# Convolution taps laid out by pairs of channels, with the two channels innermost

## The chip, the cores and the metric

The kernel runs on one core of a Trainium2 chip. The metric is device time in microseconds (us), the median of several runs. Engines are named as in the profile: PE is TensorE, DVE VectorE, ACT ScalarE, POOL GpSimd, and SP the engine that only issues transfers here. All data are float32 or rounded float32 (fp32r).

## The reference

The result mixes two branches of the same length, gated per row: a state-space convolution (an FFT in the reference) over 2048 samples and 512 channels, and a dense layer pair with gelu.

```python
g = sigmoid((u * gate_w).sum(-1, keepdims=True))            # [L, 1], L = 2048
K = einsum("dn,dnl,dn->dl", C, exp(dt * A * l), dt * B).real # taps, d = 512, n = 128
a = irfft(rfft(pad(u)) * rfft(pad(K)))[:L] + u * Dskip       # causal convolution
b = gelu(x @ w1 + b1) @ w2 + b2                              # x: 2048 x 512, w1: 512 x 1792
out = g * a + (1 - g) * b
```

The part that matters here is K: for each channel a sum over 128 states (the partitions) of products of a complex coefficient with a complex power, at 2048 sample numbers. The kernel splits a sample number into 32 coarse and 64 fine steps, so that K of one channel is a product of two tables, 32 x 128 by 128 x 64.

## The kernel before

The program has two halves. `front` makes the taps, runs the first transform stage of taps and signal, and does the whole dense branch between them; `conv` then multiplies the spectra, transforms back and adds the branches. Between the halves the first stage's results go through DRAM (`tu_d` for the signal, `tk_d` for the taps), since their rows change places.

In `front` every piece of work is a task of a planner (`Plan`) with an engine, an estimated duration, a due time out of the table DUES and the names of what it reads and writes. The planner's result is a fixed order of instructions on each engine; engines take their instructions strictly in that order and wait on semaphores where another engine has to be done first. Dense work (matmuls at lines 985 to 987 and 1028 to 1031, gelu at 1002, splits into high and low parts at 1005 and 1012) and tap work are interleaved on PE, ACT and DVE in that order.

The taps come in 4 groups of 128 channels, each in 4 chunks of CW = 32 channels, so 16 chunks. For one chunk:

- `phases` (DVE, L695 and L703) adds up 33 integer phases per channel by doubling, into `ph`, and `waves` (ACT, L711 to L713) turns them into cosines and sines in `tt`.
- `begin` (ACT, L721) copies the first four powers from `x4` into `xc[k]` (two such buffers lie in the tile den), and `powers` doubles them three times with complex products (`cmul`, DVE, L594 to L597) to 32 coarse powers. The products' temporaries `xt_` and `xv_` lie in the tile loft, as `tt` does; `zz` holds the factors.
- `magnitudes` (POOL's memset L740, DVE L752 and L750) makes 64 fine magnitudes by doubling, in both directions from the middle, and `rotate` (DVE L763, L770, L774) multiplies them by cosines and sines into `y`.
- `contract` multiplies the two tables on PE (L788): per channel two matmuls (real, imaginary), with 32 coarse powers as the weights and 64 fine samples as the moving data. Four channels stand side by side in columns of 32. A matmul's output goes to every eighth word of a PSUM tile `pks`. Each f32 matmul is two matmul records and two weight loads in the profile, so a chunk has 128 records of each; this text calls them a burst.

Behind a burst DVE adds the skip term (L804), ACT copies the result out (L807), and after every second chunk the first transform stage follows (PE L489, ACT L815). After the fourth chunk of a group eight transfers store it to `tk_d` (L830, on SP's queue, which also loads the signal's rows for the second half, L535). `conv` loads tk (L1197) and multiplies it with constants (p2k, L1218).

Before the change the channel is the innermost index of all the tables of a chunk: `y` is [2, 64, CW], `xc` [2, 32, CW], `tt` [2, 33, CW], and a factor of `cmul` is a run of 32 channels that is read again for each sample. A matmul of `contract` therefore reads its channel at a step of 32 words:

```python
x[:, r, :, ch],
y[:, r, :, ch],
```

Of the kernel before, what the change touches and what calls it, by code (L numbers as in the profile page):

```python
# [17 lines left out]
P = 128  # L18
# [331 lines left out]
def gated_mix(  # L350
# [52 lines left out]
    def front(pool, psum, keep, attic, loft, den, pr):  # L403
# [29 lines left out]
        pus = tiles(N_PU, [P, D], "pu", space=psum)  # L433

        sk = pool.tile([P, 64, 2, 4, 8], F32, name="sk")
        y = pool.tile([P, 2, 64, CW], F32, name="y")
        xc = [den[:, k : k + 4].rearrange("p k d -> p (k d)").rearrange("p (a b c) -> p a b c", a=2, c=CW) for k in (0, 4)]
        xt_, xv_ = (loft[:, k * 1024 : k * 1024 + 1024].rearrange("p (a b c) -> p a b c", a=2, c=CW) for k in range(2))
        tt = loft[:, 2048:4160].rearrange("p (a b c) -> p a b c", a=2, c=CW)
        ph = pool.tile([P, 33, CW], I32, name="phase")  # L440
        zz = pool.tile([P, 2, 5, UW], F32, name="zz")
        x4 = pool.tile([P, 2, 4, UW], F32, name="x4")
        ea = tiles(2, [P, 6, UW], "ea")
        dtb = pool.tile([P, UW], F32, name="dtb")
        ti = pool.tile([P, UW], I32, name="ti")
# [95 lines left out]
        def make_dt():  # L541

            x, k, r, ki = dts
            ki = ki.bitcast(I32)
            ln2h = 355.0 / 512.0
            v = nc.vector

            def before():
                v.tensor_scalar(k, x, 1.0 / np.log(2.0), MAGIC, ALU.mult, ALU.add)
                v.tensor_scalar(k, k, MAGIC, None, ALU.subtract)  # L550
                v.scalar_tensor_tensor(r, k, -ln2h, x, ALU.mult, ALU.add)
                v.scalar_tensor_tensor(
                    r, k, -(float(np.log(2.0)) - ln2h), r, ALU.mult, ALU.add
                )
# [12 lines left out]
            act(0.1, lambda: nc.scalar.activation(r, r, AF.Exp, scale=0.25), -200, [], ["dt"], table="exp")
            vec(400, behind, -200, [], ["dt"])
            move(2, lambda: nc.sync.dma_start(dt_d.rearrange(shape, c=4), r), D_SD, ["dt"], ["dt_d"])
            some, scaled, ones = (x4[0:32, 0, k] for k in range(3))  # L570
            pl.add("POOL", 0.1, lambda: nc.gpsimd.memset(ones, 1.0), -190, [], ["x4"])
            move(16, lambda: nc.gpsimd.dma_start(some, c1[0:32, 64:192]), -190, [], ["x4"], queue="GP")
            vec(
                UW,
                lambda: v.tensor_mul(
                    scaled.rearrange("p (a b) -> p a b", b=4),
                    some.rearrange("p (a b) -> p a b", b=4),
                    r[0:32].unsqueeze(1).to_broadcast([32, 32, 4]),
                ),
                -190, ["dt"], ["x4"],  # L580
            )
            mm(
                0.4, lambda: nc.tensor.matmul(pus[1][:, 0:UW], ones, scaled, start=True, stop=True), -190,
                ["x4"], [("pu", 1)], tiled=True,
            )
            vec(UW, lambda: v.tensor_copy(dtb, pus[1][:, 0:UW]), -190, [("pu", 1)], ["dtb"])

        def cmul(due, dst, a, br, bi, n, t, v, ka, kb, kd, kt, kv):

            w = a.shape[-1]  # L590
            br = br.unsqueeze(1).unsqueeze(1).to_broadcast([P, 2, n, w])
            bi = bi.unsqueeze(1).unsqueeze(1).to_broadcast([P, 2, n, w])
            vv, m = nc.vector, n * w
            vec(2 * m, lambda: vv.tensor_mul(t, a, br), due, [ka, *kb], [kt])  # L594
            vec(2 * m, lambda: vv.tensor_mul(v, a, bi), due, [ka, *kb], [kv])  # L595
            vec(m, lambda: vv.tensor_sub(dst[:, 0], t[:, 0], v[:, 1]), due, [kt, kv], [kd])
            vec(m, lambda: vv.tensor_add(dst[:, 1], t[:, 1], v[:, 0]), due, [kt, kv], [kd])  # L597

        sc = pr[:, 0:4]
        flat = {"xt": xt_, "xv": xv_}  # L600
        fr, rr = (
            z.rearrange("p a b c -> p (a b c)").rearrange("p (k w) -> p k w", w=UW)
            for z in (xt_, xv_)
        )

        def parts(k, n, shape):

            z = xc[k].rearrange("p a b c -> p (a b c)")[:, :n]
            return z.rearrange("p (a w) -> p a w", w=UW) if shape == 1 else z

        def prepare(u, t, eb_k):
# [53 lines left out]
        def coefficients(u, t, eb_k):  # L665
# [2 lines left out]
            v = nc.vector  # L668
            vec(5 * UW, lambda: v.tensor_mul(zz[:, 0], rr[:, 2:7], eb[:, 0:5]), t, ["xv", kx], ["zz"])
            vec(5 * UW, lambda: v.tensor_mul(zz[:, 1], fr[:, 2:7], eb[:, 0:5]), t, ["xt", kx], ["zz"])  # L670
            t1, v1, wc = (eb[:, 2 * i : 2 * i + 2].unsqueeze(2) for i in range(3))
            cmul(t, wc, sc[:, 2:4].unsqueeze(2), pr[:, 4], pr[:, 5], 1, t1, v1, "pr", [], kx, kx, kx)
            cmul(t, x4[:, :, 0:1], wc, rr[:, 1], fr[:, 1], 1, t1, v1, kx, ["xt", "xv"], "x4", kx, kx)
            cmul(
                t, x4[:, :, 1:2], x4[:, :, 0:1], zz[:, 0, 0], zz[:, 1, 0], 1, t1, v1,
                "x4", ["zz"], "x4", kx, kx,
            )
            t2, v2 = (
                z.rearrange("p a b c -> p (a b c)")[:, : 4 * UW].rearrange(
                    "p (a b c) -> p a b c", a=2, b=2  # L680
                )
                for z in (xt_, xv_)
            )
            cmul(
                t, x4[:, :, 2:4], x4[:, :, 0:2], zz[:, 0, 1], zz[:, 1, 1], 2, t2, v2,
                "x4", ["zz"], "x4", "xt", "xv",
            )

# [19 lines left out]

        def waves(t):
            def sines():  # L710
                nc.scalar.activation(tt[:, 0], ph, AF.Abs)  # L711
                nc.scalar.activation(tt[:, 1], ph, AF.Sin, scale=TWO_PI / TURN)
                nc.scalar.activation(tt[:, 0], tt[:, 0], AF.Sin, bias=half_pi, scale=-TWO_PI / TURN)  # L713

            act(3.14, sines, t + D_KA, ["ph"], ["tt"], "sin")
# [1 line left out]
        def begin(c, k, t):  # L717

            cs = slice(c * CW, (c + 1) * CW)
            act(  # L720
                0.31, lambda: nc.scalar.copy(xc[k][:, :, 0:4], x4[:, :, :, cs]), t + D_KA,  # L721
                ["x4"], [("xc", k)],
            )

        def powers(c, k, t):
            cs = slice(c * CW, (c + 1) * CW)
            x = xc[k]
            for i in range(2, 5):
# [8 lines left out]
        def magnitudes(u, c, t):  # L737

            cs = slice(c * CW, (c + 1) * CW)
            pl.add("POOL", 0.1, lambda: nc.gpsimd.memset(e[:, 63], 1.0), t, [], ["y1"])  # L740

            def both(lo, step, n):

                a = e[:, lo : lo + n].copy()
                return bass.AP(a.tensor, a.offset, [a.ap[0], [step * CW, 2], *a.ap[1:]])

            def double(k):
                n = 1 << k
                an = ea[u % 2][:, k, cs].unsqueeze(1).unsqueeze(1).to_broadcast([P, 2, n, CW])
                nc.vector.tensor_mul(both(n, 64 - 3 * n, n), both(0, 64 - n, n), an)  # L750

            vec(CW, lambda: nc.vector.tensor_copy(e[:, 0], ea[u % 2][:, 5, cs]), t, [("ea", u % 2)], ["y1"])  # L752
            for k in range(5):
                vec(2 * CW << k, lambda k=k: double(k), t, [("ea", u % 2)], ["y1"])

        def rotate(t):

            v = nc.vector
            cc = tt[:, 0, 0:32]
            cc = bass.AP(cc.tensor, cc.offset, [cc.ap[0], [CW, 2], *cc.ap[1:]])  # L760

            def real():
                v.tensor_mul(  # L763
                    y[:, 0].rearrange("p (a b) c -> p a b c", a=2),
                    e.rearrange("p (a b) c -> p a b c", a=2),
                    cc,
                )

            def imag0():
                v.scalar_tensor_tensor(e[:, 0:32], e[:, 0:32], -1.0, tt[:, 1, 0:32], ALU.mult, ALU.mult)  # L770
# [3 lines left out]
            vec(32 * CW, lambda: v.tensor_mul(e[:, 32:64], e[:, 32:64], tt[:, 1, 1:33]), t, ["tt"], ["y1"])  # L774

        pair = []

        def contract(u, c, k, t):
# [4 lines left out]
            def products(g0):  # L783
                for gg in range(g0, g0 + 4):
                    for r in range(2):
                        for j in range(4):
                            ch = j * 8 + gg
                            nc.tensor.matmul(  # L788
                                pks[q][32 * j : 32 * j + 32, :, gg],
                                x[:, r, :, ch],  # L790
                                y[:, r, :, ch],
                                start=(r == 0),
                                stop=(r == 1),
                                skip_group_check=True,
# [679 lines left out]
```

## Time and profile before

| | |
|---|---|
| runs before | 509.93, 510.2 and 507.17 us; median 509.93 |
| profiled execution: span | 505.5 us, 12181 instructions; the page gives no other time for it, and the median of the runs is 4.4 us above its span |
| PE busy | 495.2 us (98%) |
| DVE busy | 429.2 us (85%) |
| ACT busy | 365.0 us (72%) |
| matmuls of L788 | 2048 records, 61.4 us busy |
| bytes moved | 107.56 MB, mean 213 GB/s |

How to read it: a group's row gives line, engine and operation, what is written and read, the shape, then busy time and mean duration of one in ns, then the idle time ahead of it and what ended that. Matmuls overlap, so a matmul's duration is longer than its distance to the next one. A stage's row gives the busy time of each engine in it; "granted clock" (PEclk) is 1.00 at full speed.

### The profile page before, as it was taken

What the parts mean: (1) busy time and instruction counts of PE and PEld (TensorE: products, weight loads), DVE (VectorE), ACT (ScalarE), POOL (GpSimd) and SP (SyncE); (2) the same over time, 40 slices, a digit from 0 to 9 for tenths busy, and PEclk for the clock granted to TensorE, in tenths of its full rate; (3) what the DMA queues carried; (4) which work ended last, traced back from release to release, by engine and by line L of the source; (5) the groups of instructions that cost most, each with busy time, mean ns of one, the idle gap of its engine ahead of it and who ended that gap; (6) DMA issues with size and microseconds to landing.
All of it is one profiled execution on the core that took longest, in us unless ns stands there. A gap on an engine that the chain in (4) does not pass through costs nothing.

```text
span 505.5 us, 12181 instructions
## 1 busy us (share of the span) xinstructions
PE 495.2 (98%) x4802; PEld 379.0 (75%) x4802; DVE 429.2 (85%) x817; ACT 365.0 (72%) x632; POOL 38.3 (8%) x78
## 2 busy tenths in 40 slices
PE   8999999999999999999999999999999999999994
PEld 7898888898989889888988888998989522222551
DVE  4977999999999999999999999999940197877455
ACT  6999997899997789997767998636834465565310
POOL 2000000000000000001010020110100100231000
PEclk9999999999999999999999999999999999999998
DMA  8978686531858622855987244950477999989897
GB/s 286 350 280 278 188 243 213 161 126 43 280 138 246 200 73 72 254 168 116 232 217 241 75 64 128 186 100 3 154 219 169 259 389 389 338 305 391 294 344 299
DMA packets 81569, 107.56 MB, mean 213 GB/s; under 512 B 39284, under 2 KB 43784, under 8 KB 80968
## 3 DMA queue, kind: packets, MB, share of 16 engines
q1 hardware_dynamic: 74792, 82.80, 51.8%
q0 software_dynamic: 6016, 20.70, 15.4%
q10 hardware_dynamic: 704, 3.28, 1.8%
q8 instruction: 38, 0.62, 0.5%
q14 instruction: 19, 0.16, 0.1%
HBM read 61.14 MB, written 45.62 MB: 211 GB/s over the span
## 4 chain that ended last, share of the span: by engine, by line
PE 93%; DMA 2%; SPq 1%; DVE 1%; issue 1%; ACT 0%; POOL 0%; DVEq 0%; POOLq 0%
PE pk L788 12%; PE ph L985 10%; PE acc L1028 10%; PE ph L987 10%; PE ph L986 10%; PE acc L1029 9%; PE acc L1031 9%; PE p2k L1218 5%; PE p2u L1218 5%; PE pa L1257 3%; PE ph L489 3%; PE pb L1373 2%; DMA tk<-tk_d 1%; SPq L830 1%; DMA tk_d<-sk 1%; PE acc L1101 1%
## 5 line engine op out<-in xcount | busy, mean ns | idle before, releaser
L985 PE MATMUL ph<-xh,wh 128*128 128x256 f32 x448 | 127.5, 285 | 0.0
L987 PE MATMUL ph<-xh,wl 128*128 128x256 f32 x448 | 126.8, 283 | 0.0
L986 PE MATMUL ph<-xlo,wh 128*128 128x256 f32 x448 | 126.7, 283 | 0.0
L985 PEld LDWEIGHTS ph<-xh,wh 128*128 128x128 f32 x448 | 85.2, 190 | 6.9 <-issue 4.0
L986 PEld LDWEIGHTS ph<-xlo,wh 128*128 128x128 f32 x448 | 85.1, 190 | 2.1
L987 PEld LDWEIGHTS ph<-xh,wl 128*128 128x128 f32 x448 | 85.2, 190 | 0.0
L1028 PE MATMUL acc<-wh,hh 128*128 128x512 f32 x208 | 84.3, 405 | 0.0
L1029 PE MATMUL acc<-wl,hh 128*128 128x512 f32 x208 | 81.7, 393 | 0.0
L1031 PE MATMUL acc<-wh,hl 128*128 128x512 f32 x208 | 81.4, 391 | 0.0
L1002 ACT ACTIVATE ph<-ph,b1t 128x256 f32<-128x256 f32 x112 | 50.5, 451 | 25.0 <-PE ph L987 23.2
L788 PE MATMUL pk<-y,den 128*32 128x64 f32 x2048 | 61.4, 290 | 0.0
L788 PEld LDWEIGHTS pk<-y,den 128*32 128x32 f32 x2048 | 57.2, 136 | 2.6 <-issue 0.7
L1012 DVE TENSOR_TENSOR hl<-ph,hh 128x512 fp32r<-128x512 f32 (+1 forms) x62 | 38.2, 618 | 18.3 <-ACT hh L1005 10.8
L1028 PEld LDWEIGHTS acc<-wh,hh 128*128 128x128 f32 x208 | 39.1, 188 | 19.4 <-issue 8.8
L750 DVE TENSOR_TENSOR y<-y,ea 128x64 f32<-128x64 f32 (+4 forms) x80 | 45.3, 566 | 0.8 <-POOL y L740 0.3
L1031 PEld LDWEIGHTS acc<-wh,hl 128*128 128x128 f32 x208 | 39.1, 188 | 8.8
L1029 PEld LDWEIGHTS acc<-wl,hh 128*128 128x128 f32 x208 | 39.1, 188 | 6.1
L1226 ACT COPY k<-p2k 128x512 f32<-128x512 f32 x32 | 18.6, 586 | 27.2 <-issue 11.3
L594 DVE TENSOR_TENSOR loft<-den,zz 128x256 f32<-128x256 f32 (+2 forms) x48 | 37.2, 774 | 0.2
L595 DVE TENSOR_TENSOR loft<-den,zz 128x256 f32<-128x256 f32 (+2 forms) x48 | 37.2, 775 | 0.1
L763 DVE TENSOR_TENSOR y<-y,loft 128x2048 f32<-128x2048 f32 x16 | 36.6, 2286 | 0.4 <-ACT loft L713 0.2
L1005 ACT CAST hh<-ph 128x512 fp32r<-128x512 f32 (+1 forms) x62 | 33.0, 533 | 4.3 <-PE acc L1029 2.4
(197 smaller groups left out, 873.3 us busy)
## 6 DMA issues: line engine op xcount, KB each, us to landing
tk_d<-sk SPq DMA_DIRECT2D x32, 256.0 KB, 5.3
t_d<-sa SPq DMA_DIRECT2D x32, 256.0 KB, 5.1
tu_d<-attic SPq DMA_DIRECT2D x40, 128.0 KB, 3.5
attic<-in_xt_dram SPq DMA_DIRECT2D x16, 256.0 KB, 4.3
attic<-in_xs_dram SPq DMA_DIRECT2D x16, 256.0 KB, 5.0
xl_d<-xlo SPq DMA_DIRECT2D x8, 512.0 KB, 5.9
xh_d<-xh SPq DMA_DIRECT2D x8, 512.0 KB, 3.9
out_dram<-io SPq DMA_DIRECT2D x16, 256.0 KB, 3.1
```

The lines of the kernel that those rows point to most:

```text
L594: vec(2 * m, lambda: vv.tensor_mul(t, a, br), due, [ka, *kb], [kt])
L750: nc.vector.tensor_mul(both(n, 64 - 3 * n, n), both(0, 64 - n, n), an)
L788: nc.tensor.matmul(pks[q][32 * j : 32 * j + 32, :, gg], x[:, r, :, ch], y[:, r, :, ch], start=(r == 0), stop=(r == 1), skip_group_check=True,)
L985: nc.tensor.matmul(p, h, xh[xk][:, d], start=(d == 0), stop=False)
L986: nc.tensor.matmul(p, h, xlo[xk][:, d], start=False, stop=False)
L987: nc.tensor.matmul(p, lo, xh[xk][:, d], start=False, stop=(d == 3))
L1002: nc.scalar.activation(phs[q][:, n], phs[q][:, n], AF.Gelu_apprx_tanh, bias=b1t[:, f : f + 1])
L1012: nc.vector.tensor_sub(lo, phs[q][:, 0:nf], hi.bitcast(F32))
L1028: nc.tensor.matmul(a, h, wh[1][w], start=start, stop=False, skip_group_check=seeded)
L1029: nc.tensor.matmul(a, h, wl[1][w], start=False, stop=False, skip_group_check=seeded)
L1031: nc.tensor.matmul(a, l, wh[1][w], start=False, stop=stop, skip_group_check=seeded)
L1218: nc.tensor.matmul(out[64 * i : 64 * i + 64], w, x, start=True, stop=True)
```

## The change

All tables of a chunk are stored by pairs of channels (CL = 2, CH = 16 pairs): pair first, then sample, then the two channels, so `y` is [2, 16, 64, 2]. `x4` is laid out so too. One channel's samples then stand 2 words apart in place of 32. The phases `ph` and the tables ea, zz and sc keep their layout; `waves` writes from one layout into the other, and a factor is read as one pair, again and again, for all samples of the pair. The core of the diff:

```diff
+CL = 2
+CH = CW // CL
...
-        y = pool.tile([P, 2, 64, CW], F32, name="y")
+        y = pool.tile([P, 2, CH, 64, CL], F32, name="y")
...
-        x4 = pool.tile([P, 2, 4, UW], F32, name="x4")
+        x4 = pool.tile([P, 2, UW // CL, 4, CL], F32, name="x4")
...
+        def each(z, n):
+            z = z.rearrange("p (h l) -> p h l", l=CL).unsqueeze(2)
+            return z.to_broadcast([P, z.shape[1], 2 * n, CL])
+        def lines(z):
+            return z.rearrange("p a h n l -> p h a (n l)")
...
-            br = br.unsqueeze(1).unsqueeze(1).to_broadcast([P, 2, n, w])
-            bi = bi.unsqueeze(1).unsqueeze(1).to_broadcast([P, 2, n, w])
-            vec(2 * m, lambda: vv.tensor_mul(t, a, br), due, [ka, *kb], [kt])
+            br, bi = each(br, n), each(bi, n)
+            vec(2 * m, lambda: vv.tensor_mul(lines(t), lines(a), br), due, [ka, *kb], [kt])
...
-                nc.scalar.activation(tt[:, 0], ph, AF.Abs)
-                nc.scalar.activation(tt[:, 1], ph, AF.Sin, scale=TWO_PI / TURN)
+                to = [tt[:, i].rearrange("p h b l -> p b h l") for i in range(2)]
+                turns = ph.rearrange("p b (h l) -> p b h l", l=CL)
+                nc.scalar.activation(to[0], turns, AF.Abs)
+                nc.scalar.activation(to[1], turns, AF.Sin, scale=TWO_PI / TURN)
...
-                return bass.AP(a.tensor, a.offset, [a.ap[0], [step * CW, 2], *a.ap[1:]])
+                return bass.AP(a.tensor, a.offset, [a.ap[0], a.ap[1], [step * CL, 2], [1, n * CL]])
...
-                                x[:, r, :, ch],
-                                y[:, r, :, ch],
+                                x[:, r, ch // CL, :, ch % CL],
+                                y[:, r, ch // CL, :, ch % CL],
```

The instructions of every engine keep their number, order and element counts; only their shapes differ. DVE at the second chunk, where `powers` and `magnitudes` alternate (y is the fine table, ea its factors, den the coarse powers xc, loft the temporaries, zz their factors), before:

```order
L752 COPY y_95<-ea0_99 128x32
L804 TENSOR_TENSOR pk0_91<-pk0_91,dm_147 128x8
L596 TENSOR_TENSOR den_78<-loft_77 128x256
L750 TENSOR_TENSOR y_95<-y_95,ea0_99 128x2x32
L597 TENSOR_TENSOR den_78<-loft_77 128x256
L750 TENSOR_TENSOR y_95<-y_95,ea0_99 128x2x64
L594 TENSOR_TENSOR loft_77<-den_78,zz_97 128x1024
```

And the same place in the changed kernel, whose lines have other numbers:

```order
L767 COPY y_95<-ea0_99 128x16x2
L821 TENSOR_TENSOR pk0_91<-pk0_91,dm_147 128x8
L606 TENSOR_TENSOR den_78<-loft_77 128x16x16
L765 TENSOR_TENSOR y_95<-y_95,ea0_99 128x16x2x2
L607 TENSOR_TENSOR den_78<-loft_77 128x16x16
L765 TENSOR_TENSOR y_95<-y_95,ea0_99 128x16x2x4
L604 TENSOR_TENSOR loft_77<-den_78,zz_97 128x16x2x32
```

Nothing has moved; runs that were 32 words or longer are now rows of 2n words for each of 16 pairs. L788, L594 to L597, L750, L752, L763, L770, L774, L711 and L712 of the kernel before are L805, L604 to L607, L765, L767, L780, L787, L791, L726 and L727 of the changed one.

More of the change, by code (lines that the diff above doesn't have):

```diff
@@ L435, in front @@
         sk = pool.tile([P, 64, 2, 4, 8], F32, name="sk")
-        y = pool.tile([P, 2, 64, CW], F32, name="y")
-        xc = [den[:, k : k + 4].rearrange("p k d -> p (k d)").rearrange("p (a b c) -> p a b c", a=2, c=CW) for k in (0, 4)]
-        xt_, xv_ = (loft[:, k * 1024 : k * 1024 + 1024].rearrange("p (a b c) -> p a b c", a=2, c=CW) for k in range(2))
-        tt = loft[:, 2048:4160].rearrange("p (a b c) -> p a b c", a=2, c=CW)
+        y = pool.tile([P, 2, CH, 64, CL], F32, name="y")
+        xc = [den[:, k : k + 4].rearrange("p k d -> p (k d)").rearrange("p (a h b l) -> p a h b l", a=2, h=CH, l=CL) for k in (0, 4)]
+        xt_, xv_ = (loft[:, k * 1024 : k * 1024 + 1024].rearrange("p (a h b l) -> p a h b l", a=2, h=CH, l=CL) for k in range(2))
+        tt = loft[:, 2048:4160].rearrange("p (a h b l) -> p a h b l", a=2, h=CH, l=CL)
         ph = pool.tile([P, 33, CW], I32, name="phase")
         zz = pool.tile([P, 2, 5, UW], F32, name="zz")
-        x4 = pool.tile([P, 2, 4, UW], F32, name="x4")
+        x4 = pool.tile([P, 2, UW // CL, 4, CL], F32, name="x4")
         ea = tiles(2, [P, 6, UW], "ea")
@@ L569, in make_dt @@
             move(2, lambda: nc.sync.dma_start(dt_d.rearrange(shape, c=4), r), D_SD, ["dt"], ["dt_d"])
-            some, scaled, ones = (x4[0:32, 0, k] for k in range(3))
+            flat4 = x4.rearrange("p a h b l -> p (a h b l)")
+            some, scaled, ones = (flat4[0:32, k * UW : k * UW + UW] for k in range(3))
             pl.add("POOL", 0.1, lambda: nc.gpsimd.memset(ones, 1.0), -190, [], ["x4"])
@@ L586, in make_dt @@
             vec(UW, lambda: v.tensor_copy(dtb, pus[1][:, 0:UW]), -190, [("pu", 1)], ["dtb"])
-        def cmul(due, dst, a, br, bi, n, t, v, ka, kb, kd, kt, kv):
-            w = a.shape[-1]
-            br = br.unsqueeze(1).unsqueeze(1).to_broadcast([P, 2, n, w])
-            bi = bi.unsqueeze(1).unsqueeze(1).to_broadcast([P, 2, n, w])
-            vv, m = nc.vector, n * w
-            vec(2 * m, lambda: vv.tensor_mul(t, a, br), due, [ka, *kb], [kt])
-            vec(2 * m, lambda: vv.tensor_mul(v, a, bi), due, [ka, *kb], [kv])
+        def each(z, n):
[3 more added lines that the diff above has]
+            return z.rearrange("p a h n l -> p h a (n l)")
+        def cmul(due, dst, a, br, bi, n, t, v, ka, kb, kd, kt, kv):
+            vv, m = nc.vector, n * br.shape[-1]
+            br, bi = each(br, n), each(bi, n)
+            vec(2 * m, lambda: vv.tensor_mul(lines(t), lines(a), br), due, [ka, *kb], [kt])
+            vec(2 * m, lambda: vv.tensor_mul(lines(v), lines(a), bi), due, [ka, *kb], [kv])
             vec(m, lambda: vv.tensor_sub(dst[:, 0], t[:, 0], v[:, 1]), due, [kt, kv], [kd])
@@ L601, in front @@
         fr, rr = (
-            z.rearrange("p a b c -> p (a b c)").rearrange("p (k w) -> p k w", w=UW)
+            z.rearrange("p a h b l -> p (a h b l)").rearrange("p (k w) -> p k w", w=UW)
             for z in (xt_, xv_)
@@ L606, in parts @@
         def parts(k, n, shape):
-            z = xc[k].rearrange("p a b c -> p (a b c)")[:, :n]
+            z = xc[k].rearrange("p a h b l -> p (a h b l)")[:, :n]
             return z.rearrange("p (a w) -> p a w", w=UW) if shape == 1 else z
@@ L670, in coefficients @@
             vec(5 * UW, lambda: v.tensor_mul(zz[:, 1], fr[:, 2:7], eb[:, 0:5]), t, ["xt", kx], ["zz"])
-            t1, v1, wc = (eb[:, 2 * i : 2 * i + 2].unsqueeze(2) for i in range(3))
-            cmul(t, wc, sc[:, 2:4].unsqueeze(2), pr[:, 4], pr[:, 5], 1, t1, v1, "pr", [], kx, kx, kx)
-            cmul(t, x4[:, :, 0:1], wc, rr[:, 1], fr[:, 1], 1, t1, v1, kx, ["xt", "xv"], "x4", kx, kx)
+            t1, v1, wc = (
+                eb[:, 2 * i : 2 * i + 2].rearrange("p a (h l) -> p a h l", l=CL).unsqueeze(3) for i in range(3)
+            )
+            sc4 = sc[:, 2:4].rearrange("p a (h l) -> p a h l", l=CL).unsqueeze(3)
+            cmul(t, wc, sc4, pr[:, 4], pr[:, 5], 1, t1, v1, "pr", [], kx, kx, kx)
+            cmul(t, x4[:, :, :, 0:1], wc, rr[:, 1], fr[:, 1], 1, t1, v1, kx, ["xt", "xv"], "x4", kx, kx)
             cmul(
-                t, x4[:, :, 1:2], x4[:, :, 0:1], zz[:, 0, 0], zz[:, 1, 0], 1, t1, v1,
+                t, x4[:, :, :, 1:2], x4[:, :, :, 0:1], zz[:, 0, 0], zz[:, 1, 0], 1, t1, v1,
                 "x4", ["zz"], "x4", kx, kx,
@@ L678, in coefficients @@
             t2, v2 = (
-                z.rearrange("p a b c -> p (a b c)")[:, : 4 * UW].rearrange(
-                    "p (a b c) -> p a b c", a=2, b=2
+                z.rearrange("p a h b l -> p (a h b l)")[:, : 4 * UW].rearrange(
+                    "p (a h b l) -> p a h b l", a=2, b=2, l=CL
                 )
@@ L684, in coefficients @@
             cmul(
-                t, x4[:, :, 2:4], x4[:, :, 0:2], zz[:, 0, 1], zz[:, 1, 1], 2, t2, v2,
+                t, x4[:, :, :, 2:4], x4[:, :, :, 0:2], zz[:, 0, 1], zz[:, 1, 1], 2, t2, v2,
                 "x4", ["zz"], "x4", "xt", "xv",
@@ L720, in begin @@
             act(
-                0.31, lambda: nc.scalar.copy(xc[k][:, :, 0:4], x4[:, :, :, cs]), t + D_KA,
+                0.31, lambda: nc.scalar.copy(xc[k][:, :, :, 0:4], x4[:, :, c * CH : c * CH + CH]), t + D_KA,
                 ["x4"], [("xc", k)],
@@ L730, in powers @@
                 cmul(
-                    t, x[:, :, n : 2 * n], x[:, :, 0:n], zz[:, 0, i, cs], zz[:, 1, i, cs], n,
-                    xt_[:, :, 0:n], xv_[:, :, 0:n], ("xc", k), ["zz"], ("xc", k), "xt", "xv",
+                    t, x[:, :, :, n : 2 * n], x[:, :, :, 0:n], zz[:, 0, i, cs], zz[:, 1, i, cs], n,
+                    xt_[:, :, :, 0:n], xv_[:, :, :, 0:n], ("xc", k), ["zz"], ("xc", k), "xt", "xv",
                 )
@@ L739, in magnitudes @@
             cs = slice(c * CW, (c + 1) * CW)
-            pl.add("POOL", 0.1, lambda: nc.gpsimd.memset(e[:, 63], 1.0), t, [], ["y1"])
+            pl.add("POOL", 0.1, lambda: nc.gpsimd.memset(e[:, :, 63], 1.0), t, [], ["y1"])
             def both(lo, step, n):
-                a = e[:, lo : lo + n].copy()
-                return bass.AP(a.tensor, a.offset, [a.ap[0], [step * CW, 2], *a.ap[1:]])
+                a = e[:, :, lo : lo + n].copy()
+                return bass.AP(a.tensor, a.offset, [a.ap[0], a.ap[1], [step * CL, 2], [1, n * CL]])
             def double(k):
                 n = 1 << k
-                an = ea[u % 2][:, k, cs].unsqueeze(1).unsqueeze(1).to_broadcast([P, 2, n, CW])
+                an = each(ea[u % 2][:, k, cs], n)
                 nc.vector.tensor_mul(both(n, 64 - 3 * n, n), both(0, 64 - n, n), an)
-            vec(CW, lambda: nc.vector.tensor_copy(e[:, 0], ea[u % 2][:, 5, cs]), t, [("ea", u % 2)], ["y1"])
+            vec(CW, lambda: nc.vector.tensor_copy(
+                    e[:, :, 0], ea[u % 2][:, 5, cs].rearrange("p (h l) -> p h l", l=CL)
+                ), t, [("ea", u % 2)], ["y1"])
             for k in range(5):
@@ L758, in rotate @@
             v = nc.vector
-            cc = tt[:, 0, 0:32]
-            cc = bass.AP(cc.tensor, cc.offset, [cc.ap[0], [CW, 2], *cc.ap[1:]])
+            cc = tt[:, 0, :, 0:32]
+            cc = bass.AP(cc.tensor, cc.offset, [cc.ap[0], cc.ap[1], [CL, 2], [1, 32 * CL]])
             def real():
                 v.tensor_mul(
-                    y[:, 0].rearrange("p (a b) c -> p a b c", a=2),
-                    e.rearrange("p (a b) c -> p a b c", a=2),
+                    y[:, 0].rearrange("p h (a b) l -> p h a (b l)", a=2),
+                    e.rearrange("p h (a b) l -> p h a (b l)", a=2),
                     cc,
@@ L769, in imag0 @@
             def imag0():
-                v.scalar_tensor_tensor(e[:, 0:32], e[:, 0:32], -1.0, tt[:, 1, 0:32], ALU.mult, ALU.mult)
+                v.scalar_tensor_tensor(e[:, :, 0:32], e[:, :, 0:32], -1.0, tt[:, 1, :, 0:32], ALU.mult, ALU.mult)
             vec(64 * CW, real, t, ["tt", "y1"], ["y0"])
             vec(32 * CW, imag0, t, ["tt"], ["y1"])
-            vec(32 * CW, lambda: v.tensor_mul(e[:, 32:64], e[:, 32:64], tt[:, 1, 1:33]), t, ["tt"], ["y1"])
+            vec(32 * CW, lambda: v.tensor_mul(e[:, :, 32:64], e[:, :, 32:64], tt[:, 1, :, 1:33]), t, ["tt"], ["y1"])
         pair = []
@@ L1072, in dense @@
             sks = sk.rearrange("p a b c d -> p (a b c d)").rearrange("p (f a b) -> p f a b", a=2, b=D)
-            ys = y.rearrange("p a b c -> p (a b c)").rearrange("p (f a b) -> p f a b", a=2, b=D)
+            ys = y.rearrange("p a h b l -> p (a h b l)").rearrange("p (f a b) -> p f a b", a=2, b=D)
             x = load_x(0, -300)
```

## Prediction

> **What bounds the kernel now.** I read the chain that ended last by engine, then the busy time by stage (below its heading the stages from 60 and from 376 us), then the chain in order of time.
>
> ```profile
> PE 93%; DMA 2%; SPq 1%; DVE 1%; issue 1%; ACT 0%; POOL 0%; DVEq 0%; POOLq 0%
> ```
>
> ```profile
> core 0: us, PE busy (x) PEld busy (x) DVE busy (x) ACT busy (x) POOL busy (x), PEclk, DMA share, GB/s
> 60.00:376.00 316.00, 316.00 (x3782) 274.74 (x3770) 305.15 (x579) 257.60 (x433) 21.77 (x44) 1.00 0.57 158
> 376.00:402.00 26.00, 25.32 (x186) 19.99 (x176) 3.79 (x7) 11.11 (x23) 1.71 (x2) 1.00 0.81 190
> ```
>
> By the first line this is a TensorE kernel. The stages say more. From 60 to 376 us, where the taps are made, PE is never free, but DVE works 305.15 of 316 us as well: the two are level. So whatever PE saves here, DVE lets through only what DVE itself waits, 10.85 us in all, gaps between instructions included. From 376 us on DVE is nearly idle, then PE and the DMA queues set the pace. The way between the two stages is the chain at the last of the 16 bursts of line 788:
>
> ```profile
> 372.81 3.76 PE pk L788 x127
> ...
> 396.56 5.76 DMA tk<-tk_d
> 402.36 2.49 PE p2k L1218 x8
> ```
>
> The last burst feeds the first transform stage (L489), its result goes to tk_d and back as tk, and the second half starts at 402.36 with p2k. I found no wait in it that is not counted from the end of that burst, and PE's dense work behind the burst (25.32 of 26 us busy) moves with it too. So an earlier end of the last burst moves everything behind it, one for one. The term to find is how much earlier.
>
> **What the burst costs, and why.** The change leaves all orders as they are; only addresses differ. PE reads one channel of y and xc: 128 bytes from word to word before, 8 bytes after.
>
> ```profile
> 71.61 3.84 PE L788 MATMUL pk<-y,den 128*32 128x64 f32 x128
> 75.38 0.50 PE L1028 MATMUL acc<-wh,hh 128*128 128x512 f32 x1
> ```
>
> ```profile
> L788 PE MATMUL pk<-y,den 128*32 128x64 f32 x2048 | 61.4, 290 | 0.0
> L788 PEld LDWEIGHTS pk<-y,den 128*32 128x32 f32 x2048 | 57.2, 136 | 2.6 <-issue 0.7
> ...
> L1218 PE MATMUL p2u<-attic,f 128*64 128x512 f32 x32 | 9.2, 592 | 0.0
> ...
> L1373 PEld LDWEIGHTS pb<-t,g1t 128*64 128x64 f32 x52 | 3.7, 137 | 7.0 <-issue 4.9 <-DVE loft L1386 1.4 <-DVE attic L1386 0.3
> ```
>
> ```profile
> L583 PE MATMUL pu<-x x2: 270/321/372, 12.5 to 12.7; 32*128 32x128 f32 x2
> ```
>
> A burst holds PE for 75.38 - 71.61 = 3.77 us: 128 matmuls, four side by side in columns of 32, so 32 rounds of 118 ns. Contiguous f32 matmuls give the price of a column: 512 take 592 ns and 128 take 270 (the shorter of L583's two), (592 - 270)/384 = 0.84 ns each. 64 columns should thus stream in 54 ns, and a matmul should last 216 ns; L788 has 290. The weights say the same: 32 scattered columns load in 136 ns, as long as 64 contiguous ones (137). Reading at 128 bytes costs about double. **At 8 bytes** no row shows PE. Bounds: 32 rounds of 54 ns plus the last matmul's way out, about 1.9 us a burst, or 3.77 as now. 8 bytes is nearer to the 4 of the contiguous rows than to 128, so I take 1.9, a saving of 1.9 us; 16 bursts would free 30 us of PE.
>
> [...]
>
> **From PE's 30 us to the end.** PE may run ahead only until y is ready.
>
> ```profile
> 369.29 1.22 DVE L774 TENSOR_TENSOR y<-y,loft 128x1024 f32<-128x1024 f32 x1
> ...
> 374.43 0.69 DVE L1012 TENSOR_TENSOR hl<-ph,hh 128x512 fp32r<-128x512 f32 x1 [3.32 <-ACT hh L1005]
> ```
>
> ```profile
> 372.74 3.83 PE L788 MATMUL pk<-y,den 128*32 128x64 f32 x128
> ```
>
> ```profile
> DVE hl L1012 <- ACT hh L1005: 4.5, 5, 3.3
> DVE pk L804 <- PE pk L788: 2.5, 6, 0.6
> ```
>
> The last rotation ends at 369.29 + 1.22 = 370.51; the burst begins at 372.74, so **2.2 us** are PE's lateness. They go: burst 15 alone gives 1.9 of them, the 14 before it leave more than the rest. The burst itself gives **1.9 us**. Third, DVE's own waits: 2.5 us for the bursts (L804 adds to pk at once behind each), and 4.5 - 3.3 = 1.2 us for hh, since the wait of 3.3 lies behind the last rotation. Nothing to 3.7 us can come back; ACT also works in order and 257.6 of 316 us, so I count only the waits on bursts, **2.5 us**. Sum: 6.6 us, out of bounds of 0 and 7.8. What is late next is DVE, and PE then waits some 24 us in the stage.
>
> **What it adds.** DVE runs the same instructions on as many elements, with factors now read as repeated pairs and rows of 2n words in place of 32:
>
> ```profile
> L750 DVE TENSOR_TENSOR y<-y,ea 128x64 f32<-128x64 f32 (+4 forms) x80 | 45.3, 566 | 0.8 <-POOL y L740 0.3
> ...
> L595 DVE TENSOR_TENSOR loft<-den,zz 128x256 f32<-128x256 f32 (+2 forms) x48 | 37.2, 775 | 0.1
> L594 DVE TENSOR_TENSOR loft<-den,zz 128x256 f32<-128x256 f32 (+2 forms) x48 | 37.2, 774 | 0.2
> L763 DVE TENSOR_TENSOR y<-y,loft 128x2048 f32<-128x2048 f32 x16 | 36.6, 2286 | 0.4 <-ACT loft L713 0.2
> ...
> L596 DVE TENSOR_TENSOR den<-loft 128x128 f32<-128x128 f32 (+2 forms) x48 | 22.3, 465 | 0.4
> L597 DVE TENSOR_TENSOR den<-loft 128x128 f32<-128x128 f32 (+2 forms) x48 | 22.2, 463 | 0.0
> L770 DVE SCALAR_TENSOR_TENSOR y<-y,loft 128x1024 f32<-128x1024 f32 x16 | 19.5, 1220 | 0.0
> L774 DVE TENSOR_TENSOR y<-y,loft 128x1024 f32<-128x1024 f32 x16 | 19.5, 1219 | 0.0
> ```
>
> ```profile
> L712 ACT ACTIVATE loft<-phase 128x1056 f32<-128x1056 int32 x16 | 17.5, 1094 | 0.2
> ...
> L815 ACT COPY sk<-pu 128x512 f32<-128x512 f32 x16 | 8.9, 600 | 5.4 <-PE pu L489 5.4
> ...
> L507 ACT COPY attic<-pu 128x512 f32<-128x512 f32 x11 | 6.3, 602 | 0.4 <-PE pu L489 0.4
> ```
>
> These eight groups are 240 us, and DVE has no room: each per cent is 2.4 us on the end. Bounds: nothing, or PE's doubling, +240 us. The nearest row is on ACT: L815 writes runs of 8 words with gaps as fast (600 ns) as L507 without any (602). I take 0. ACT's L712, and L711 of the same size, now write pairs with gaps, 35 us in all; at worst doubled, 58.4 us of free time in the stage would hide most. The copy den<-x4 and POOL's memset stay small.
>
> [...] No row here shows runs of two.
>
> 505.5 - 6.6 = 498.9 us of span. The page gives the profiled execution no other time than its span; the median of the runs, 509.9, lies 4.4 above it. With the same 4.4 I get **503.3 us**.
>
> **Rivals.**
> - *The matmul is held by its output.* L788 writes pk at a step of 8 words, and that stays. If this, not the read, makes 118 ns a round, bursts stay near 3.77 us and the time at 509.9 (508 to 512). Against it: weights, which write nothing, are doubled too. For it: no other matmul writes with gaps, so no row parts the two. It is also the case in which the change doesn't do what it says. [...]
> - *Half way:* rounds of about 86 ns, a burst near 2.8. Then 2.2 + 1.0 + about 1.5 = 4.7 us: 505.2.
> - *The clock takes it back.* PE now waits in the stage, and the granted clock falls where PE is idle:
>
> ```profile
> 494.00:506.00 12.00, 4.93 (x28) 1.72 (x24) 5.97 (x10) 0.00 (x0) 0.00 (x0) 0.80 0.73 278
> ```
>
>   If waits come in long pieces, the bursts behind them run slowly and PE arrives late as before; only a part of 1.9 + 2.5 is left: about 507. Against it: with 24 us over 16 bursts a piece is some 1.5 us.
> - *Slower: pairs cost DVE (or ACT).* From 6.6/2.4 = 2.8% on the eight groups on, the gain is gone; at 5% it is 503.3 + 12 = 515 us, since DVE paces the stage.
>
> **How the numbers follow.** About 1% (5 us) is what can be told from no change; the runs before span 507.2 to 510.2. Forecast 0.50 (own range 500 to 506), held by its output 0.26, half way 0.09, clock 0.05, slower 0.10. Faster by over 1% means below 504.8: 0.8 of the forecast, half of half way, together 0.45. Slower 0.10, the rest 0.45 within 1%. The range 499.5 to 512 takes in the whole gain and the unchanged burst, and leaves the slower case out.
>
> **What would show it.** In the changed profile the matmul of the burst near 220 ns and the burst near 1.9 us; DVE's groups with the same means; waits of PE on y's last rotation where there were none; the last burst starting right behind it, at 366 to 370 us. I am wrong if the burst keeps 3.7 us, if TENSOR_TENSOR of 1024 elements leaves 1219 ns, or if the burst shrinks and the end does not move with the last rotation.

## The result, and the profile after

The changed kernel takes **501.55 us** (median of 4 runs, 500.09 to 502.67) against 509.49 us of the kernel before (median of 4 runs beside it): ratio **0.9856, 95% interval 0.9821 to 0.9891**, 5.6 to 9.1 us less. 503.3 us was forecast. The profiled execution has a span of 500.4 us, 5.1 less than before. (One execution of a kernel in the table below, at a granted clock of 0.66, took 658 us, and that kernel's median is taken without it.)

The chain that ended last, by engine, in the profile after:

```profile
PE 32%; DVE 31%; ACT 22%; issue 6%; DMA 6%; SPq 3%; POOL 0%; DVEq 0%; ACTq 0%; POOLq 0%
```

Where 93% of the chain was PE, three engines now share it: 32% of its time is matmuls, 31% products of DVE and 22% work of ACT. The busy time by stage, in the columns shown before:

```profile
60.00:376.00 316.00, 301.81 (x3828) 251.90 (x3827) 305.37 (x582) 263.47 (x439) 21.80 (x44) 1.00 0.59 161
376.00:402.00 26.00, 25.81 (x151) 18.74 (x149) 5.18 (x9) 11.50 (x26) 1.71 (x2) 1.00 0.87 217
```

PE has free time in the stage, 14 us where there was none; DVE's 305.37 us are what they were (305.15). The granted clock is 1.00. What PE waits for there (who waits, for whom, us in total, times, longest us):

```profile
PE acc L1048 <- DVE hl L1029: 3.5, 5, 1.1
PE ph L1002 <- DVE hl L1029: 2.4, 3, 1.3
PE ph L491 <- DVE hl L1029: 2.3, 2, 1.4
...
PE pk L805 <- DVE y L791: 1.1, 2, 0.5
```

hh and hl are the high and the low part of the dense branch's data; ACT makes the first, and DVE then the second. So PE waits mostly for DVE, 8.2 us for hl and only 1.1 for the rotation's last product. The groups of instructions (line, engine, shapes, count, then busy us, mean ns, and idle time before them):

```profile
L765 DVE TENSOR_TENSOR y<-y,ea 128x64 f32<-128x64 f32 (+4 forms) x80 | 45.2, 565 | 0.6
...
L604 DVE TENSOR_TENSOR loft<-den,zz 128x256 f32<-128x256 f32 (+2 forms) x48 | 37.1, 772 | 0.1
...
L805 PE MATMUL pk<-y,den 128*32 128x64 f32 x2048 | 35.0, 223 | 1.3 <-DVE y L791 1.1
...
L726 ACT ACTIVATE loft<-phase 128x1056 f32<-128x1056 int32 x16 | 19.8, 1237 | 1.5 <-DVE phase L708 1.5
L727 ACT ACTIVATE loft<-phase 128x1056 f32<-128x1056 int32 x16 | 19.6, 1227 | 0.2
...
L791 DVE TENSOR_TENSOR y<-y,loft 128x1024 f32<-128x1024 f32 x16 | 19.5, 1216 | 0.0
```

L805 (L788 before) fell from 61.4 to 35.0 us and from 290 to 223 ns. L765, L604 and L791 (L750, L594 and L774 before) kept their means within 0.3%. L726 and L727 (L711 and L712 before) did not: 1093 and 1094 ns became 1237 and 1227.

The first burst and the last one in the timeline of PE (start us, us, work):

```profile
72.86 2.13 PE L805 MATMUL pk<-y,den 128*32 128x64 f32 x128
74.92 0.50 PE L1045 MATMUL acc<-wh,hh 128*128 128x512 f32 x1
...
368.45 2.15 PE L805 MATMUL pk<-y,den 128*32 128x64 f32 x128
370.89 0.39 PE L1002 MATMUL ph<-xh,wh 128*128 128x256 f32 x1 [0.29 <-DVE hl L1029]
```

A burst holds PE for 74.92 - 72.86 = 2.06 us, not 3.77. The last one begins at 368.45; before, it began at 372.74. DVE's waits in the stage now end with

```profile
DVE hl L1029 <- ACT hh L1022: 2.6, 3, 1.9
```

in first place. The wait for the bursts (2.5 us at L804 before) has left the list; the one for hh fell from 4.5 to 2.6, of which the longest piece (3.3 before, 1.9 now) lies behind the last rotation.

One row serves to compare all kernels below: the timeline of the 16 rotations' last product, with the start of the first and of the last. Before and after:

```profile
L774 DVE TENSOR_TENSOR y<-y,loft x16: 1216/1219/1223, 59.2 to 369.3; 128x1024 f32<-128x1024 f32 x16
```

```profile
L791 DVE TENSOR_TENSOR y<-y,loft x16: 1208/1216/1222, 60.4 to 366.5; 128x1024 f32<-128x1024 f32 x16
```

From the first to the last rotation lie 310.1 us before and 306.1 after: DVE's way through the stage, free of what happened ahead of it. Here it shortened by 4.0 us.

### The profile page after: what moved, and what is told of

The parts are those of the page before. It is cut to its first block, busy times and chain, and to the rows that moved or that the text cites. A ratio compares the mean times of both kernels' runs of the same rounds, so it can differ in the third digit from the quotient of the medians.

```text
span 500.4 us, 12185 instructions
## 1 busy us (share of the span) xinstructions
PE 477.4 (95%) x4802; PEld 354.1 (71%) x4802; DVE 428.1 (86%) x817; ACT 368.4 (74%) x632; POOL 38.3 (8%) x78
## 4 chain that ended last, share of the span: by engine, by line
PE 32%; DVE 31%; ACT 22%; issue 6%; DMA 6%; SPq 3%; POOL 0%; DVEq 0%; ACTq 0%; POOLq 0%
PE p2k L1235 5%; PE p2u L1235 5%; DVE loft L605 4%; DVE loft L604 4%; DVE y L780 4%; DVE y L765 3%; PE pa L1274 3%; ACT ph L1019 3%; DVE hl L1029 3%; ACT L1019 3%; PE ph L1002 2%; DVE phase L708 2%; PE ph L1004 2%; PE ph L1003 2%; DVE den L607 2%
## 5 line engine op out<-in xcount | busy, mean ns | idle before, releaser
L765 DVE TENSOR_TENSOR y<-y,ea 128x64 f32<-128x64 f32 (+4 forms) x80 | 45.2, 565 | 0.6
L780 DVE TENSOR_TENSOR y<-y,loft 128x2048 f32<-128x2048 f32 x16 | 36.6, 2285 | 0.8 <-ACT loft L728 0.6
L604 DVE TENSOR_TENSOR loft<-den,zz 128x256 f32<-128x256 f32 (+2 forms) x48 | 37.1, 772 | 0.1
L805 PE MATMUL pk<-y,den 128*32 128x64 f32 x2048 | 35.0, 223 | 1.3 <-DVE y L791 1.1
L805 PEld LDWEIGHTS pk<-y,den 128*32 128x32 f32 x2048 | 31.8, 110 | 4.4 <-issue 2.2
```

Source lines behind the costliest of these rows:

```text
L604: vec(2 * m, lambda: vv.tensor_mul(lines(t), lines(a), br), due, [ka, *kb], [kt])
L780: v.tensor_mul(y[:, 0].rearrange("p h (a b) l -> p h a (b l)", a=2), e.rearrange("p h (a b) l -> p h a (b l)", a=2), cc,)
L805: nc.tensor.matmul(pks[q][32 * j : 32 * j + 32, :, gg], x[:, r, ch // CL, :, ch % CL], y[:, r, ch // CL, :, ch % CL], start=(r == 0), stop ...
```

## The experiments

The table gives, for each kernel, how long the first burst holds PE, the way from the first to the last rotation, and the time against the kernel before in the same session.

| kernel | burst us | rotations us | median us | ratio, 95% interval |
|---|---|---|---|---|
| before | 3.77 | 310.1 | 507.7 to 509.5 | 1 |
| after | 2.06 | 306.1 | 501.55 | 0.986 [0.982, 0.989] |
| groups of 4 channels | 4.06 | 314.1 | 511.74 | 1.008 [1.005, 1.010] |
| groups of 1 channel | 1.94 | 329.2 | 526.60 | 1.038 [1.034, 1.041] |
| groups of 8 channels | 4.20 | 317.0 | 515.12 | 1.015 [1.012, 1.017] |
| before, output in a row | 3.76 | 310.1 | 507.71 | 1.000 [0.998, 1.001] |
| before, half bursts | 1.95 | 304.6 | 500.52 | 0.985 [0.983, 0.987] |
| after, half bursts | 1.10 | 306.1 | 503.28 | 0.990 [0.988, 0.992] |
| before, DVE relieved | 3.77 | 309.1 | 508.15 | 0.999 [0.997, 1.001] |
| after, DVE relieved | 2.07 | 298.7 | 494.49 | 0.974 [0.969, 0.978] |
| after, ACT writes in a row | 2.06 | 304.6 | 500.49 | 0.986 [0.983, 0.989] |
| y alone by pairs | 2.20 | 306.2 | 502.18 | 0.989 [0.987, 0.991] |
| after, product on POOL | 2.05 | - | 511.88 | 1.008 [1.005, 1.010] |
| after, copies on POOL | 2.07 | 305.4 | 500.89 | 0.987 [0.985, 0.989] |

### At which step does the read become slow?

```diff
-CL = 2
+CL = 4        # then 1, then 8
```

> Same program as the changed kernel, groups of four channels in place of pairs: PE reads a channel at a step of 16 bytes. If what counts is how many words of a 16-byte stretch are used (theory A: two are enough, one is not), the burst is as long as before the change, 3.7 to 3.8 us, a matmul 290 ns, a weight load 136 ns, and the time goes back to about 509 us. If the cost grows gradually with the step (theory B), the burst lies between, 2.3 to 2.9 us, matmul 235 to 260 ns, time 503 to 506 us. DVE means should stay within 1% by both.

> Groups of one channel: PE reads a channel contiguously (4 bytes). Theory A: nothing left to gain on the read, burst 2.0 to 2.1 us, matmul 223 ns, weight load 110 ns. Theory B: a little shorter, 1.9 us, matmul near 216 ns. ACT's waves then write single words at a step of 33 words: 1240 ns as in the changed kernel if a gap costs the same whatever it is, towards 2200 ns if each gap costs. DVE reads one repeated word as factor: means within 1% if nothing of its step counts. Time 500 to 502 us if DVE and ACT hold, 505 or more if either does not.

> Groups of eight channels: PE reads a channel at a step of 32 bytes. Theory A: as the step of 16 bytes and as before the change, burst 3.7 to 3.8 us, time about 509 us. Theory B: longer than at 16 bytes, burst 2.9 to 3.4 us, time 506 to 508 us.

The groups of the kernels with four, eight and one channel, in this order; the third begins with one product of L604, and the last row, by itself, is the same product in the changed kernel:

```profile
L805 PE MATMUL pk<-y,den 128*32 128x64 f32 x2048 | 65.9, 302 | 0.0
L805 PEld LDWEIGHTS pk<-y,den 128*32 128x32 f32 x2048 | 61.5, 140 | 2.6 <-ACT attic L509 0.4 <-issue 0.4
```

```profile
L805 PE MATMUL pk<-y,den 128*32 128x64 f32 x2048 | 68.8, 310 | 0.0
L805 PEld LDWEIGHTS pk<-y,den 128*32 128x32 f32 x2048 | 64.4, 146 | 2.6 <-issue 0.7
```

```profile
L604 DVE TENSOR_TENSOR den<-x,zz 128x256 f32<-128x256 f32 x4 | 2.6, 650 | 0.0
...
L726 ACT ACTIVATE loft<-phase 128x1056 f32<-128x1056 int32 x16 | 36.1, 2254 | 1.0 <-DVE phase L708 1.0
...
L805 PE MATMUL pk<-y,den 128*32 128x64 f32 x2048 | 32.8, 220 | 3.9 <-DVE y L791 2.1 <-ACT attic L509 1.7
```

```profile
L604 DVE TENSOR_TENSOR den<-x,zz 128x256 f32<-128x256 f32 x4 | 1.7, 421 | 0.0
```

By the step of the read the burst takes 1.94 us (4 bytes), 2.06 (8), 4.06 (16), 4.20 (32) and 3.77 (128, before). The jump lies between 8 and 16 bytes, as theory A said; a gradual rise (theory B) would have put 16 bytes between 2.3 and 2.9. But A was not right in all: 16 and 32 bytes cost more than 128, and the times follow that. Sixteen bursts longer by 0.29 and 0.43 us make 4.6 and 6.9 us; the medians rose by 3.7 and 7.0 us over those of before beside them. Where PE paces the stage, a microsecond of bursts is about one of time (0.8 and 1.0 here).

What makes the jump is not shown: theory A's stretch of 16 bytes was the author's assumption, and nothing in it tells 16 and 32 bytes from 128.

With single channels PE gained another 0.12 us a burst, and far more was lost elsewhere. ACT's waves took 2254 ns, and DVE's waits in that kernel, from 60 to 390 us, begin with

```profile
DVE hl L1029 <- ACT hh L1022: 7.5, 8, 2.4
DVE phase L716 <- ACT loft L727: 5.4, 7, 1.4
```

DVE's products over single words with gaps (den<-x,zz) rose from 421 to 650 ns; those over long rows of single channels stayed (L604 with 1024 elements: 1217 ns in both). So of the sizes tried a pair is the smallest group that costs DVE nothing, and also the largest that PE reads fast. On DVE's side, den<-x,zz reads pairs with gaps in 421 ns, and in 420 before the change, where its rows had none.

### Is it the output?

```diff
-pks = tiles(N_PK, [P, 64, 8], "pk", space=psum)
+pks = tiles(N_PK, [P, 8, 64], "pk", space=psum)
-    pks[q][32 * j : 32 * j + 32, :, gg],
+    pks[q][32 * j : 32 * j + 32, gg],
```

> The kernel before the change, its burst now writing each channel's 64 results contiguously in PSUM (step of 1 word in place of 8); ACT's copy of the result reads it transposed instead. If the read sets the burst (the prediction's theory), the burst stays at 3.6 to 3.8 us, matmul about 290 ns, and the time at 509 to 511 us (ACT's 16 copies may cost a little more). If the output sets it (the rival), the burst falls to 2 us or less, matmul below 225 ns, and the time to about 502 us, with the old layout of y and xc.

```profile
L788 PE MATMUL pk<-y,den 128*32 128x64 f32 x2048 | 61.4, 290 | 0.0
```

Not one figure of the row moved. The rival, to which the prediction gave 0.26, is out. No run has both a fast read and an output in a row, so a small cost beside the fast read isn't ruled out, though the 220 ns of single channels, with gaps in the output, are close to the prediction's 216. ACT's copy that now reads pk transposed took 586 ns, as before (587), so its gaps cost nothing either.

### Is it PE's time alone, and who is late next?

```diff
-for r in range(2):          # both kernels: half of each burst
+for r in range(1):
```

> The kernel before the change with half of each burst: the 64 matmuls of the imaginary parts are left out (the result lacks them), the layout and all else stay, DVE and ACT included. A burst should take 3.77/2 = 1.9 us. If the change gained through PE's time in the bursts alone (the prediction's theory), this kernel must come out like the changed one, ratio 0.983 to 0.988 (501 to 502 us), with the last rotation 2 to 3 us earlier than before. If the layout gained elsewhere (DVE, ACT, the transfers), it stays nearer to before, ratio over 0.99.

> The changed kernel with half of each burst (imaginary parts left out, as in the kernel above). A burst should take about 1.05 us, so PE has another 16 us. If DVE paces the stage after the change, nearly none of them arrives: only the last burst's own 1.0 us and the PE lateness of 0.8 us ahead of it, 500 to 501 us, ratio 0.981 to 0.985. If PE still paced the stage, 490 us or less.

```diff
-e[:, 0:32], e[:, 0:32], -1.0, tt[:, 1, 0:32]      # both kernels
+e[:, 0:1], e[:, 0:1], -1.0, tt[:, 1, 0:1]
```

> The kernel before the change with DVE relieved of 18 us: of the rotation's second product (16 times 1.22 us) only 1 of 32 samples is done (the result is wrong for the others). If PE paces the stage before the change, as the prediction read it, nothing is gained: ratio 0.995 to 1.0, PE without a free moment from 60 to 376 us, the rotation ending far ahead of the burst. If DVE paced it, 490 to 495 us.

> The changed kernel with DVE relieved in the same way. PE is busy 297.6 of 311 us up to the last burst, so it can give at most 13 us. If DVE is what is late after the change, most of that comes: 488 to 493 us, ratio 0.96 to 0.97, PE without free time in the stage. If something else holds PE there (ACT, the transfers), the time stays at 500 to 502 us.

The old layout with half of its bursts (each still at 291 ns a matmul) gives 0.985, the same as the change. So shorter bursts explain the whole gain, whatever shortens them. (The last rotation began 5.6 us earlier, not the 2 to 3 expected.) The rotations of this kernel and of the changed one with half bursts:

```profile
L774 DVE TENSOR_TENSOR y<-y,loft x16: 1215/1218/1221, 59.1 to 363.7; 128x1024 f32<-128x1024 f32 x16
```

```profile
L791 DVE TENSOR_TENSOR y<-y,loft x16: 1214/1217/1224, 59.6 to 365.7; 128x1024 f32<-128x1024 f32 x16
```

A second halving took another 15 us of PE's work away and moved no rotation: 306.1 us as in the changed kernel. PE no longer paces. The median, expected at 500 to 501 us, even reads 1.7 us higher than the changed kernel's; the intervals of the two ratios overlap, and the span of its profile was 499.7 us, so I read it as no gain. The other pair, with DVE relieved (stage from 60 to 376 us, before the change and after it):

```profile
60.00:376.00 316.00, 316.00 (x3759) 274.28 (x3762) 291.51 (x579) 258.01 (x434) 21.90 (x44) 1.00 0.58 158
```

```profile
60.00:376.00 316.00, 306.96 (x3873) 259.84 (x3872) 291.64 (x582) 265.51 (x444) 21.78 (x44) 0.99 0.60 165
```

Fourteen microseconds less of DVE's work in the stage bought nothing before the change (0.999): PE stays at 316.00. After it they bought 7 us more. 494.49 us lies above the 488 to 493 expected, and PE, at 306.96 of 316 us, isn't full: DVE's first wait in that kernel is now

```profile
DVE hl L1029 <- ACT hh L1022: 8.7, 11, 2.9
```

where it was 2.6 (up to the last rotation 5.9 and 0.7). That points to ACT (265.51 of 316 us busy, in the planner's fixed order) as the next in line; no run relieved ACT there.

### What ACT's gapped writes cost, and which operand counts

```diff
-to = [tt[:, i].rearrange("p h b l -> p b h l") for i in range(2)]
-turns = ph.rearrange("p b (h l) -> p b h l", l=CL)
+to = [tt[:, i].rearrange("p h b l -> p (h b l)") for i in range(2)]
+turns = ph.rearrange("p b c -> p (b c)")
```

> The changed kernel, but ACT's two waves L726 and L727 write their 1056 words in a row, as before the change, not as pairs with gaps (so the phases lie at wrong places). Their means should go back from 1237 and 1227 ns to 1093. If these longer writes are what lay between the changed kernel and the old layout with half a burst (first to last rotation 306.1 us there, 304.7 here), the rotations now take 304.7 us and the time is 500 to 501 us, ratio 0.981 to 0.986. If ACT's time is hidden, the rotations stay at 306.1 us and the time at 501 to 502 us.

```profile
L726 ACT ACTIVATE loft<-phase 128x1056 f32<-128x1056 int32 x16 | 17.5, 1092 | 1.7 <-DVE phase L708 1.7
```

```profile
L791 DVE TENSOR_TENSOR y<-y,loft x16: 1204/1216/1222, 60.1 to 364.7; 128x1024 f32<-128x1024 f32 x16
```

1092 ns are back, and the rotations take 304.6 us, exactly as in the old layout with half bursts. So the longer writes, 4.5 us of ACT, cost the stage 1.5 us that were not hidden. In the time (0.986 both) this can't be told apart.

```diff
-xc = [... "p (a h b l) -> p a h b l", a=2, h=CH, l=CL ...]
+xc = [... "p (a h b l) -> p a h b l", a=2, h=1, l=32 ...]      # likewise xt_, xv_, x4
```

> Half of the change: y and its factors tt lie by pairs, xc, its factors and x4 in the old layout. So PE streams y at a step of 8 bytes and loads its weights at 128. If the streamed operand alone sets the burst, the matmul goes to 223 ns, the burst to 2.0 to 2.2 us, the weight load stays at 136 ns, time 501 to 502 us. If the weight loads set it, the burst stays at 3.7 us and 509 us. If both count, something like 2.8 us and 505 us.

```profile
L805 PE MATMUL pk<-y,den 128*32 128x64 f32 x2048 | 37.4, 229 | 0.9 <-DVE y L791 0.8
...
L805 PEld LDWEIGHTS pk<-y,den 128*32 128x32 f32 x2048 | 34.6, 140 | 3.9 <-issue 1.6 <-ACT attic L509 0.4
```

With weights that still load in 140 ns, the burst takes 2.20 us. Of the 1.71 us gained, y alone gives 1.57; the weights add 0.14.

### Two attempts at a faster version

```diff
-vec(32 * CW, lambda: v.tensor_mul(e[:, :, 32:64], ...
+vec(32 * CW, lambda: nc.gpsimd.tensor_mul(e[:, :, 32:64], ...
```

> A version meant to be faster: the changed kernel with one product of the rotation (L791, 16 times 1.22 us) given from DVE to POOL, which works 21.8 of 316 us in the stage; all orders stay. If DVE is what is late after the change and POOL takes about as long, DVE loses 19.5 us and the time falls to 493 to 497 us, as where the other product was left out. Against it: POOL's products may take several times as long, may slow DVE beside them, or wait in POOL's queue behind the transfers L1083 and L926, which wait for ACT and PE there; then the bursts come late and the time is 502 to 515 us.

```profile
L791 POOL TENSOR_TENSOR y<-y,loft 128x1024 f32<-128x1024 f32 x16 | 53.7, 3355 | 89.5 <-DVE y L780 61.3 <-ACT st L509 14.5 <-DVE ti L664 13.1
...
L604 DVE TENSOR_TENSOR loft<-den,zz 128x256 f32<-128x256 f32 (+2 forms) x48 | 42.2, 880 | 0.2
L787 DVE SCALAR_TENSOR_TENSOR y<-y,loft 128x1024 f32<-128x1024 f32 x16 | 21.5, 1341 | 0.0
```

POOL takes 3355 ns in the mean (2191 to 5958) where DVE took 1216, and while it works DVE's products get longer (L604 from 772 to 880, L787 from 1217 to 1341). 511.9 us: a loss.

```diff
-nc.vector.tensor_copy(e[:, :, 0], ...)
+nc.gpsimd.tensor_copy(e[:, :, 0], ...)      # right behind POOL's memset
-to, turns: written "p b h l"
+to, turns: read "p h b l", written in a row
```

> A version meant to be faster, from what the runs showed: the changed kernel with DVE's 16 copies of the first magnitudes (L767, 174 ns each, 2.8 us) given to POOL right behind its memset there, and ACT's waves L726 and L727 writing their words in a row while they read the phases by pairs, with the right values in the right places. If DVE paces, first to last rotation (306.1 us) gets shorter by the 2.8 us and by the 1.1 us that the gapped writes cost: 302 to 303 us, and the time is 497 to 499 us, ratio 0.977 to 0.982. Against it: gapped reads may cost ACT as much as gapped writes (1237 ns), which leaves 1.1 us out; POOL's copy of 32 words may come later than DVE's did and hold the first doubling, then nothing or less than nothing is left of the 2.8 us, 501 us or more.

```profile
L726 ACT ACTIVATE loft<-phase 128x1056 f32<-128x1056 int32 x16 | 19.7, 1231 | 1.2 <-DVE phase L708 1.1
...
L756 POOL COPY y<-ea 128x32 f32<-128x32 f32 x16 | 9.9, 616 | 4.2 <-ACT ea L653 4.2
```

Gapped reads cost ACT what gapped writes do (1231 ns at L726 for 1237), so that half fell out. Of DVE's copies little came back either: the rotations take 305.4 us, 0.7 less, where 302 to 303 were expected. The timeline of DVE in the changed kernel shows why:

```profile
95.91 0.16 DVE L821 TENSOR_TENSOR pk<-pk,dm 128x8 f32<-128x8 f32 x1
95.98 0.18 DVE L767 COPY y<-ea 128x32 f32<-128x32 f32 x1
96.07 0.68 DVE L606 TENSOR_TENSOR den<-loft 128x512 f32<-128x512 f32 x1
```

The copy begins 0.09 us before the one ahead of it ends, and the next one 0.09 us before the copy does. A copy recorded with 174 ns holds the next one up by about 90 only, 1.5 us for all 16. The version stands level with the change (500.89 us, 0.987), not at the 497 to 499 us expected.

## Why the prediction was right, point by point

**The bound.** PE paced the stage with DVE level behind it: shown from both sides, by relieving DVE before the change (no gain) and by halving bursts (the whole gain in the old layout, none in the new).

**The burst.** 2.06 us for the 1.9 forecast, 223 ns for 216. The price of a column from contiguous matmuls was a sound basis: with y and xc contiguous the burst takes 1.94. That 8 bytes would cost hardly more than 4 was the author's estimate, which no row of before shows; at 8 bytes the burst takes those 2.06. The weight load pointed to the read rightly, but it was not doubled (136 ns before, 110 by pairs and 110 contiguous), and its own share is 0.14 us.

**The sum to the end.** Before the change PE's work behind the last burst began with

```profile
376.50 0.38 PE L985 MATMUL ph<-xh,wh 128*128 128x256 f32 x1
```

From the first rotation's last product to this work lay 376.50 - 59.2 = 317.3 us before and 370.89 - 60.4 = 310.5 after: 6.8 us, where 6.6 were forecast. That the two are so close is partly luck, since the terms came otherwise. Of the 2.2 us of PE's lateness 0.8 are left (367.7 to 368.45), 1.4 gained. The last burst gave 1.3 and not 1.9, since PE then waits for hl until 370.89. The way between the rotations gave 4.0 and not 2.5. DVE's listed waits on that way fell from 4.4 to 1.7 us: the 2.5 for the bursts went, as forecast, 0.5 of those for hh (1.2 to 0.7) and 0.3 for POOL, while waits for ACT's waves and xh grew by 0.6. The other 1.3 us lie in DVE's busy time (303.4 to 302.4) and in gaps too short for the list. The layout did not shorten that busy time, for with half bursts in the old layout it is 302.2; its cause was not tried. By the ACT experiment 5.5 us would have gone without the longer writes, more than the 3.7 that the prediction set as the most.

**PE's waits.** DVE is late next, as forecast, but with hl more than with the rotation's last product (8.2 and 1.1 us), and PE is free for 14 us of the stage, not 24. From the first burst to the work behind the last one PE's busy time fell by 20.3 us (304.9 to 284.6), where 16 bursts save 27.4; why the rest of it stays busy is not shown.

**Costs taken as nothing.** Right for DVE's eight groups (565 ns for 566 at L765, 1216 for 1219 at L791). Wrong for ACT: the prediction kept L711 and L712 at their price and trusted ACT's free time to hide most of what might come. Pairs cost 12 to 13%, 4.5 us in all, and 1.5 us of it were not hidden.

**From the burst to the end one for one.** Not quite. The chain in order of time after the change:

```profile
373.59 0.76 issue
374.34 1.08 PE pu L491 x7
...
379.82 1.34 SPq L847
...
392.39 6.11 DMA tk<-tk_d
398.54 1.95 PE p2k L1235 x6
```

The first transform stage begins 5.6 us earlier than before (372.57 against 378.20), but its products into pu stop for 0.76 us and then run one after another. The stores at L847 come 4.3 us earlier, and p2k 3.8. From ACT's first copy behind p2k (404.88 before, 400.51 after) to DVE's last products all lies 4.4 us earlier. The end of the span gained 5.1, because the last output landed 3.8 us after its issue and not 4.5. That the change has a part in that is not shown. In both kernels with half bursts the products into pu run side by side without a pause; with ACT's writes in a row the pause is 0.26 us. What makes the pause is open: the profile names no wait.

**Span and median.** The span missed by 1.5 us (500.4 for 498.9), partly since its first rotation lay 1.2 us later than before; in the table's other kernels, but for those with single channels and with the product on POOL, it began at 59.0 to 60.1 us. The 4.4 us added for the median were too many. In each of the four runs after, the time lies 1.8 us above the span of its own execution; 505.5 and 1.8 make 507.3, so the profiled execution before was probably the shortest of its runs (507.17), and the 4.4 held that difference too. The median after lies 1.2 us above the profiled span. The two misses offset one another in part, which is luck; so the forecast came within 1.8 us.

**The rivals.** Held by its output: out, 290 ns a matmul with the step of 8 words and without. Half way: out. The clock: out, 1.00 in the stage. Slower by pairs: DVE shows none of it, ACT a little.

## What to carry to other kernels

When two engines are level, a saving on the one that paces is worth what the other one loses in waits, plus what lies between its last piece of work and the handover; so look at the waits of the second engine, and expect the next saving on the first to bring nothing. A layout is chosen for all its readers and writers: here, of the sizes tried, a pair of words was the one group that PE reads fast and DVE takes at no cost, and ACT paid 12 to 13% for it. Before an operation is moved to an idle engine, price it there (POOL took 3355 ns for DVE's 1216), and price what it does to its neighbour (1341 ns for 1217 at DVE's L787).

## What the runs showed of the hardware that was not expected

- PE's read of f32 words is not slowest at the widest step: a burst takes 4.20 us at 32 bytes, 4.06 at 16, but 3.77 at 128. The cause was not tried.
- Results of a matmul eight words apart in PSUM cost nothing where the scattered read sets the pace (290 ns with the step and without).
- ACT over 1056 words: 1092 ns in a row and also writing fours with gaps, 1237 writing pairs with gaps, 1231 reading them, 2254 writing single words.
- A product of 1024 words takes POOL 3355 ns in the mean (2191 to 5958), DVE 1216, and beside POOL's DVE's own L787 takes 1341.
- DVE's records in the changed kernel overlap by 70 to 90 ns from 93.5 to 98 us, so that the busy time of the shortest counts them about double (174 ns recorded, about 90 of delay to the next).
